# Work-ahead matmuls moved behind the attention output, exps issued behind the sines, and theta's whole turns taken off by an integer copy from ScalarE

## The chip, the cores and the metric

The kernel runs on one core of one Trainium2 chip. The metric is the device time of one execution in microseconds. The engines are TensorE (PE: matmul; PEld: its weight load), VectorE (DVE), ScalarE (ACT), GpSimd (POOL) and SyncE (SP), which issues the DMAs. Each engine works through its own instructions in the order in which they were issued, and stands still when the next one has to wait.

## The reference

Three layers, for 4 batches of 448 tokens, 12 heads of 64 and a width of 768:

```python
# attention
scores = scale * q @ k.T;  scores = where(causal mask, -1e9, scores)
attn = exp(scores - max);  attn = attn / (sum(attn) + 1e-9)
x = (attn @ v), heads side by side                    # (4, 448, 768)
# gated layer
gate_pre = causal convolution of x along the tokens, 5 taps, per channel
h = sigmoid(gate_pre) * (x @ w_val);   x = h @ w_out
# rotation layer
theta = x @ w_theta
y = w_tok_r @ (x * cos(theta)) + w_tok_i @ (x * sin(theta))   # mixes tokens
u = x + y;   out = u + max(u @ w_ch, 0)
```

## The kernel before, in words

Activations stand channels by tokens, a tile of 128x448 per sixth of the width. Each operand of a dense product is split into a high part of fewer bits and the remainder (`x_hi`, `x_lo`; `act_hi`, `act_lo`; `w_hl`), and a product is three matmuls a chunk: hi·hi, hi·lo, lo·hi. An output tile of a dense product is 36 matmuls of 448 columns (`gemm`, L535). The inputs arrive as 64-bit floats; weights are brought to 32 bits in integer arithmetic (`to_f32`, L167), split by POOL and stored for later batches.

**Attention** runs over 24 pairs of heads (`attn_iter(g)`, ten steps a pair). For pair g: `attn_T` transposes q and k, ACT copies `qt`, DVE `kt`; `attn_S` makes the scores in two groups (S0: chunks of 448, 320 and 128 columns; S1: 384, 192, 64 and 256), DVE masks them and takes the row maximum (L355), and ACT takes the exp into `prob` with the row sums (`exp_set`, L126). In the next pair's iteration `attn_PT` transposes `prob` in four parts, `attn_AV` multiplies by v, `attn_X1` scales the result into `xf`, splits it into `x_hi` (ACT, L470) and `x_lo` (POOL, L119), and `attn_X2` convolves it (for the first six pairs on POOL, L486 to L493) and takes the gate's tanh on ACT, also through `exp_set`. PSUM has two banks for dense products (`mm`) and six for all else.

**Work ahead.** Batch 0's attention (pairs 0 to 5) runs alone at the start, while the first weights are converted. There the first two output tiles of `x @ w_val` grow along, one chunk kc at a time (`gemm_ahead(kc)`, L506: 6 matmuls, L514). The loop at L732 takes one attention step for each n and issues chunk kc at n = 19, 29, ..., 69, just behind the pair's `attn_X` and so behind the first half of the next pair's program. How these matmuls are finally placed among PE's others is decided by the scheduler of the tile framework, which orders each engine's instructions by its own model of times; `tc.issue_after(ins)` forbids it to put what is under it ahead of `ins`.

**Dense work** is `dense(b)` for the batches in turn: 6 tiles of `x @ w_val` times the gate (`hf`, L573), 6 of `h @ w_out` (`x2f`), 6 of theta, then per tile the transposes of z (`ztr`, L617), the token mixing (`tok`, L638) and 6 tiles of the output. The loop at L753 interleaves the next batch's attention steps by the rates of `RATE`.

**Theta.** `theta(e)` takes theta/2π off PSUM with an ACT copy (L590), finds the whole turns by adding and taking off 12582912 on DVE (L591), takes them off (L592), and makes the absolute value on DVE in batch 0 (L594) and on ACT in the others (L598). The sine takes the signed fraction, the cosine the absolute one. After every second tile `sines(e-1)` issues four sines (two tiles; L610, L611), behind the last two exps that were issued (L606). The products with x follow on DVE (L614) and POOL or DVE (L615). ACT has the exp and the sine in different tables: between an exp or tanh and a sine there is an `ACT_TABLE_LOAD`, shown at L610 (to sines) or L127 (back to exps). The profile has 30 of them.

Of the kernel before, what the change touches and what calls it, by code (L numbers as in the profile page):

```python
# [11 lines left out]
I32 = mybir.dt.int32  # L12
U32 = mybir.dt.uint32
AF = mybir.ActivationFunctionType
ALU = mybir.AluOpType
# [3 lines left out]
MASKED = -8.0e9  # L19
INV_2PI = 1.0 / (2.0 * math.pi)  # L20
TWO_PI = 6.283185
ROUND = 12582912.0

U_DVE = (0, 1, 1, 1)
PT_DVE = (2, 4, 0, 0)
# [22 lines left out]
def kernel(  # L48
# [14 lines left out]
    nc = tc.nc  # L63
    B, H, S, D = q.shape
# [15 lines left out]
    KC = DM // P  # L80
# [22 lines left out]
    halfpi = cpool.tile([P, 1], F32, name="halfpi")  # L103
# [7 lines left out]
    def psum(tag):  # L111
        at = "mm" if tag == "mm" else "at"
        return ps.tile([P, 512], F32, tag=at, name=f"ps_{tag}", bufs=2 if tag == "mm" else 6)
# [8 lines left out]
        return nc.vector.tensor_tensor(out=dst, in0=src, in1=f32(hi), op=ALU.subtract)  # L122

    exps = []

    def exp_set(*args, **kw):  # L126
        exps.append(nc.scalar.activation(*args, **kw))  # L127

    def setup():
        make_identity(nc, ident)  # L130
# [24 lines left out]
    def setup_conv():  # L155
        t = pool.tile([P, CV, 2], I32, tag="wb", name="cv_raw", bufs=8)
        nc.sync.dma_start(
            out=t[: KW * KC, 0:P, :].rearrange("p n two -> p (n two)"),
            in_=conv_w.rearrange("k (c n) -> (k c) n", n=2 * P),
        )  # L160
        c32 = pool.tile([P, S], F32, tag="tmp", name="c32")[:, 0:P]
        to_f32(c32[: KW * KC, :], t[: KW * KC, 0:P, :])
        pt = psum("tr")
        nc.tensor.transpose(pt[:, : KW * KC], c32[: KW * KC, :], ident[: KW * KC, : KW * KC])
        nc.vector.tensor_copy(cw.rearrange("p k c -> p (k c)"), pt[:, : KW * KC])
# [118 lines left out]
    wides = {}  # L284
    ttr_ins = []
    hf_ins = []

    def load_qk(g, name):
        if g >= B * NP:
            return  # L290
        b, hp = divmod(g, NP)
        src, raw = (q, q_raw) if name == "q" else (k, k_raw)
        t = pool.tile([CP, NC, 2, D], F32, tag=f"{name}_raw", name=f"{name}_raw")
        for j in range(2):
            nc.sync.dma_start(out=t[:, :, j, :], in_=src[b, 2 * hp + j].rearrange("(c p) d -> p c d", p=CP))
        raw[g] = t
# [34 lines left out]
    def side(i, j):  # L331
        return j if 1 <= i <= 4 else 1 - j
# [50 lines left out]
    def attn_AV(g):  # L383
        if not 0 <= g < B * NP:
            return
        tv = v_raw.pop(g)
        t = pT.pop(g)
        av[g] = psum("av")
        for kc, lo, hi, n0 in SEGS:
            for j in range(2):  # L390
                o = side(lo, j) * D
                nc.tensor.matmul(  # L392
                    av[g][j * D : (j + 1) * D, lo * D : hi * D], lhsT=tv[:, j, kc, :],
                    rhs=t[:, n0 : n0 + hi - lo, o : o + D],
                    start=(kc, lo) == (0, 1), stop=kc == NC - 1, skip_group_check=True,
                )

    def attn_X(g):
        if not 0 <= g < B * NP:
            return  # L400
        attn_X1(g)
        attn_X2(g)
# [103 lines left out]
    def gemm_ahead(kc):  # L506
        xhi, xlo = x_hl[0, kc]
        g = kc // KH
        for n in range(AHEAD):
            if kc == 0:  # L510
                ahead[n] = psum("mm" if n < 2 else "tr")
            whi, wlo = splits[n, g]
            for m, (a, x) in enumerate(((whi, xhi), (whi, xlo), (wlo, xhi))):
                nc.tensor.matmul(  # L514
                    ahead[n][:, :S], lhsT=a[:, kc % KH, :], rhs=x,
                    start=kc == 0 and m == 0, stop=kc == KC - 1 and m == 2, skip_group_check=True,
                )
            if kc == KC - 1:
                splits.pop((n, 0)), splits.pop((n, 1))
# [35 lines left out]
    def dense(b):  # L555
# [8 lines left out]
        for e in range(KC):  # L564
            if b == 0 and e < AHEAD:
                pt = ahead.pop(e)
                if YLD:
                    yield
            else:
                pt = yield from gemm(xs)  # L570
# [3 lines left out]
                    out=hf, in0=gates.pop((b, e)), scalar=1.0, in1=pt[:, :S], op0=ALU.add, op1=ALU.mult  # L574
# [4 lines left out]
        for e in range(KC):  # L579
            pt = yield from gemm(h_hl)  # L580
# [5 lines left out]
        def theta(e):  # L586
            pt = yield from gemm(x2_hl)
            z = pool.tile([P, 2, S], F32, tag="z", name="z", bufs=4)
            t, kk = z[:, 1, :], z[:, 0, :]
            nc.scalar.activation(t, pt[:, :S], AF.Copy, scale=INV_2PI)  # L590
            nc.vector.tensor_scalar(out=kk, in0=t, scalar1=ROUND, scalar2=ROUND, op0=ALU.add, op1=ALU.subtract)  # L591
            nc.vector.tensor_tensor(out=t, in0=t, in1=kk, op=ALU.subtract)  # L592
            if ABS_DVE[b]:
                nc.vector.tensor_scalar(  # L594
                    out=kk.bitcast(I32), in0=t.bitcast(I32), scalar1=0x7FFFFFFF, scalar2=None, op0=ALU.bitwise_and
                )
            else:
                nc.scalar.activation(kk, t, AF.Abs)  # L598
            zri[e] = z
            if e % 2:  # L600
                sines(e - 1)
            yield

        def sines(e0):
            with ExitStack() as st:
                for ins in exps[-PIN:]:  # L606
                    st.enter_context(tc.issue_after(ins.ins))
                for e in (e0, e0 + 1):
                    t, kk = zri[e][:, 1, :], zri[e][:, 0, :]
                    nc.scalar.activation(t, t, AF.Sin, scale=TWO_PI)  # L610
                    nc.scalar.activation(kk, kk, AF.Sin, bias=halfpi, scale=-TWO_PI)  # L611
            for e in (e0, e0 + 1):
                t, kk = zri[e][:, 1, :], zri[e][:, 0, :]
                nc.vector.tensor_tensor(out=kk, in0=kk, in1=x2f[e], op=ALU.mult)  # L614
                (nc.vector if Z_DVE[b] else nc.gpsimd).tensor_tensor(out=t, in0=t, in1=x2f[e], op=ALU.mult)  # L615
# [58 lines left out]
        for e in range(KC):  # L674
            pt = yield from gemm(u_hl)
            nc.vector.scalar_tensor_tensor(
                out=x2f[e], in0=pt[:, :S], scalar=0.0, in1=x2f[e], op0=ALU.max, op1=ALU.add
# [54 lines left out]
    for n in range(5 * H + 10):  # L732
        next(at, None)
        if n == 5:
            setup_conv()
        if W_AT <= n < 5 * H:
            with tc.issue_after(ttr_ins[-1].ins):
                for at_n, (m, g) in zip(A_TILES, ((0, 0), (1, 0), (0, 1), (1, 1), (2, 0), (2, 1), (3, 0), (3, 1))):
                    if n == at_n - W_AT:
                        load_w(m, g)  # L740
                    if n == at_n:
                        stage_w(m, g)
                        if m < AHEAD + 1:
                            split_w(m, g)
        if n >= 19 and n % 10 == 9:
            gemm_ahead(n // 10 - 1)
        if n == 5 * H - 3:
            with tc.issue_after(ttr_ins[-1].ins):
                for g in range(2):
                    load_w(AHEAD + 2, g)  # L750
# [47 lines left out]
```

## Time and profile before

| | |
|---|---|
| median of three runs | 743.29 us (742.01 to 743.30) |
| the profiled execution's own time | 738.0 us |
| its span in the trace | 736.2 us |
| granted TensorE clock, mean | 0.977 |
| busy: PE, DVE, ACT, POOL | 93%, 57%, 51%, 43% of the span |

The span runs from the first to the last instruction that the profiler recorded. A granted clock of 1.0 is TensorE at 2.4 GHz, 0.5 is 1.2 GHz; a mean between is a mixture. Times in the rows are microseconds from the span's start; in square brackets stands how long the engine had been idle before the instruction, and the work that ended the wait.

### The profile page before, as it was taken

Reading aid. Unit: us, or ns where it says so; the run is one execution under the profiler, and the core shown is the slowest. Engines: PE = TensorE matmul, PEld = TensorE weight load, DVE = VectorE, ACT = ScalarE, POOL = GpSimd, SP = SyncE. Lnnn points to the kernel's source line nnn. Section 1 sums busy time; section 2 is a strip of 40 time slices with the busy share of each in tenths; the row PEclk is TensorE's granted clock in tenths of the full one; section 3 lists DMA queues with packets and bytes.
Section 4 is the critical chain, followed back from the end, with each engine's and each line's share of the span. In section 5 each row is a group of like instructions: output and inputs, shape, how many; then the busy total and the mean of one; then the engine's idle time right before and its main releaser. Section 6 shows DMA issues by size and latency. Waiting matters only on the chain.

```text
span 736.2 us, 13020 instructions
## 1 busy us (share of the span) xinstructions
PE 686.0 (93%) x4595; PEld 588.5 (80%) x4595; DVE 418.9 (57%) x1018; ACT 373.0 (51%) x853; POOL 314.4 (43%) x332
## 2 busy tenths in 40 slices
PE   5878897898899999999998999999999999999997
PEld 3655675787688888888887888888889899898996
DVE  5655689877876663644656534734578323126521
ACT  4655656775986454564864232444867212235301
POOL 1596954984757666662547200012331503102100
PEclk9897999999899999999999999999999999999999
DMA  7846346778553489888522268666431278773232
GB/s 199 193 99 187 93 134 194 246 206 302 165 157 119 124 298 307 265 286 263 158 76 62 75 200 242 185 191 201 121 88 58 64 216 233 213 209 97 86 98 63
DMA packets 133031, 124.68 MB, mean 169 GB/s; under 512 B 72905, under 2 KB 110567, under 8 KB 132967
## 3 DMA queue, kind: packets, MB, share of 16 engines
q1 hardware_dynamic: 132967, 123.86, 57.0%
q8 instruction: 36, 0.59, 0.3%
q14 instruction: 28, 0.23, 0.1%
HBM read 94.66 MB, written 29.16 MB: 168 GB/s over the span
## 4 chain that ended last, share of the span: by engine, by line
PE 62%; ACT 7%; DVE 4%; POOL 2%; DMA 1%; issue 1%; SPq 0%; DVEq 0%; ACTq 0%; POOLq 0%
PE ps_mm L535 35%; PE ps_mm L638 12%; PE ps_s L347 4%; PE ps_tr L370 3%; PE ps_av L392 3%; ACT L610 2%; PE ps_tr L624 2%; PE ps_tr L665 1%; PE ps_tr L320 1%; ACT L127 1%; ACT prob L127 1%; ACT z L610 1%; ACT z L611 1%; POOL gate L493 1%; DVE z L592 1%; DMA rb<-rows 1%
## 5 line engine op out<-in xcount | busy, mean ns | idle before, releaser
L535 PE MATMUL ps_mm<-act_hi,w_hl 128*128 128x448 f32 x864 | 268.5, 376 | 7.4 <-POOL w_hl L119 2.3
L535 PEld LDWEIGHTS ps_mm<-act_hi,w_hl 128*128 128x128 f32 x864 | 162.1, 189 | 26.1 <-POOL w_hl L119 5.7
L535 PE MATMUL ps_mm<-act_lo,w_hl 128*128 128x448 f32 x432 | 157.3, 364 | 0.0
L127 ACT ACTIVATE prob<-ps_s,negm 128x192 f32<-128x192 f32 (+6 forms) x168 | 79.3, 474 | 75.5 <-DVE negm L355 73.9
L355 DVE CUSTOM_DVE_ANT_0 ps_s<-ps_s,mask 128x192 f32<-128x192 f32 (+6 forms) x168 | 70.6, 436 | 70.1 <-PE ps_s L347 39.4
L535 PEld LDWEIGHTS ps_mm<-act_lo,w_hl 128*128 128x128 f32 x432 | 81.8, 189 | 4.5
L535 PE MATMUL ps_mm<-x_hi,w_hl 128*128 128x448 f32 x264 | 82.6, 379 | 0.6 <-DVE hf L573 0.4
L119 POOL TENSOR_TENSOR act_lo<-x2f,act_hi 128x448 fp32r<-128x448 f32 x36 | 41.8, 1161 | 75.8 <-ACT act_hi L549 26.3
L119 POOL TENSOR_TENSOR w_hl<-cv_raw,w_hl 128x384 fp32r<-128x384 f32 x62 | 65.3, 1054 | 18.7 <-ACT w_hl L248 17.1
L119 POOL TENSOR_TENSOR x_lo<-xf,x_hi 128x448 fp32r<-128x448 f32 x23 | 29.5, 1283 | 97.5 <-ACT x_hi L470 97.5
L638 PE MATMUL ps_mm<-wtok_h,zt_h 128*128 128x448 f32 x168 | 64.7, 385 | 2.0 <-ACT zt_h L629 1.9
L638 PE MATMUL ps_mm<-wtok_h,zt_l 128*128 128x448 f32 x168 | 63.3, 379 | 2.4 <-DVE zt_l L122 2.4
L638 PE MATMUL ps_mm<-wtok_l,zt_h 128*128 128x448 f32 x168 | 62.4, 372 | 0.0
L347 PE MATMUL ps_s<-kt,qt 64*64 64x256 f32 (+6 forms) x672 | 57.3, 416 | 4.9 <-ACT x_hi L470 1.3
L493 POOL TENSOR_TENSOR gate<-gate,tp 128x448 f32<-128x448 f32 x48 | 58.4, 1217 | 2.3
L615 POOL TENSOR_TENSOR z<-z,x2f 128x448 f32<-128x448 f32 x18 | 21.9, 1219 | 85.4 <-ACT z L610 85.4
L370 PE MATMUL ps_tr<-ident,prob 128*128 128x128 f32 x384 | 56.2, 285 | 1.4 <-ACT prob L127 1.4
L347 PEld LDWEIGHTS ps_s<-kt,qt 64*64 64x64 f32 x672 | 30.6, 140 | 32.3 <-issue 18.9
L535 PEld LDWEIGHTS ps_mm<-x_hi,w_hl 128*128 128x128 f32 x264 | 50.4, 192 | 6.3 <-DVE hf L573 0.9
L370 PEld LDWEIGHTS ps_tr<-ident,prob 128*128 128x128 f32 x384 | 47.2, 146 | 7.0 <-ACT prob L127 1.8
L392 PEld LDWEIGHTS ps_av<-pt,v 128*64 128x64 f32 x768 | 41.0, 140 | 12.9 <-DVE cv_raw L177 3.0
L392 PE MATMUL ps_av<-pt,v 128*64 128x64 f32 (+3 forms) x768 | 48.8, 281 | 2.6 <-DVE cv_raw L177 2.6
(106 smaller groups left out, 1185.8 us busy)
## 6 DMA issues: line engine op xcount, KB each, us to landing
w_hl<-scratch SPq DMA_DIRECT2D x120, 384.0 KB
scratch<-w_hl SPq DMA_DIRECT2D x48, 384.0 KB
q_raw<-in_q_dram SPq DMA_DIRECT2D x48, 112.0 KB
k_raw<-in_k_dram SPq DMA_DIRECT2D x48, 112.0 KB
out_dram<-o SPq DMA_DIRECT2D x24, 224.0 KB
v<-in_v_dram SPq DMA_DIRECT2D x48, 96.0 KB
cv_raw<-in_moe_w_val_dram SPq DMA_DIRECT2D x12, 384.0 KB
plain<-cv_raw SPq DMA_DIRECT2D x24, 192.0 KB
```

What stands on the lines that cost most here:

```text
L119: nc.gpsimd.tensor_tensor(out=dst, in0=src, in1=f32(hi), op=ALU.subtract)
L127: exps.append(nc.scalar.activation(*args, **kw))
L347: nc.tensor.matmul(bank[o : o + D, off : off + n], lhsT=qt[j * D : (j + 1) * D, i * D : (i + 1) * D], rhs=kt[j * D : (j + 1) * D, :n], sta ...
L355: ttr = nc.vector.tensor_tensor_reduce(out=pt, in0=pt, in1=mask[:, S - n : S], scale=-1.0 / math.sqrt(D), scalar=3.0e38, op0=ALU.add, op1= ...
L370: nc.tensor.transpose(pt[:, n * P : (n + 1) * P], probs[i][:, kc * P : (kc + 1) * P], ident)
L392: nc.tensor.matmul(av[g][j * D : (j + 1) * D, lo * D : hi * D], lhsT=tv[:, j, kc, :], rhs=t[:, n0 : n0 + hi - lo, o : o + D], start=(kc, l ...
L493: nc.gpsimd.tensor_tensor(out=gt, in0=gt, in1=tp, op=ALU.add)
L535: nc.tensor.matmul(pt[:, :S], lhsT=a[:, kc % KH, :], rhs=x, start=kc == 0 and m == 0, stop=kc == KC - 1 and m == 2,)
L610: nc.scalar.activation(t, t, AF.Sin, scale=TWO_PI)
L615: (nc.vector if Z_DVE[b] else nc.gpsimd).tensor_tensor(out=t, in0=t, in1=x2f[e], op=ALU.mult)
L624: nc.tensor.transpose(pt[:, (m - m0) * P : (m - m0 + 1) * P], z.rearrange("p a s -> p (a s)")[:, m * P : (m + 1) * P], ident,)
L638: nc.tensor.matmul(pt[:, :S], lhsT=a[:, m, :], rhs=w[:, m, :], start=m == 0 and n == 0, stop=m == NZ - 1 and n == 2,)
```

## The change

Three parts.

1. **Work ahead.** Chunks 0 to 4 are issued at n = 24, 34, 44, 54, 64 and no longer at 19, 29, ..., 59, and not ahead of the last matmul of the attention output (`attn_AV`) that stands in the program at that point. Chunk 5 stays at n = 69.
2. **Exps behind sines.** Every exp and tanh that goes through `exp_set` once a sine has been issued may not be put ahead of the latest cosine.
3. **Theta.** The ACT copy off PSUM writes theta/2π as int32, so that the conversion rounds to whole turns. One DVE instruction then computes theta/2π from PSUM once more and takes the integer off. The add-and-subtract of 12582912 (L591) is gone, 24 instructions in all.

On PE, part 1 shows at every pair of the first stage. Before, around pair 1, the chunk stands between the transposes of `prob` and the next scores:

```order
L370 MATMUL ps_tr<-ident,prob_77 128x128 x4
L370 MATMUL ps_tr<-ident,prob_72 128x128
L370 MATMUL ps_tr<-ident,prob_75 128x128 x3
L514 MATMUL ps_mm<-x_hi,w_ahead 128x448 x2
L347 MATMUL ps_s<-kt,qt 64x448 x2
L347 MATMUL ps_s<-kt,qt 64x320 x2
```

Now the whole chunk stands behind the attention output, ahead of the transposes of the next q and k:

```order
L396 MATMUL ps_av<-pt,v_79 64x128 x2
L396 MATMUL ps_av<-pt,v_79 64x64 x2
L396 MATMUL ps_av<-pt,v_79 64x128 x2
L396 MATMUL ps_av<-pt,v_79 64x64 x2
L519 MATMUL ps_mm<-x_hi,w_ahead 128x448
L519 MATMUL ps_mm<-x_lo,w_ahead 128x448
L519 MATMUL ps_mm<-x_hi,w_ahead 128x448 x2
L519 MATMUL ps_mm<-x_lo,w_ahead 128x448
L519 MATMUL ps_mm<-x_hi,w_ahead 128x448
L324 MATMUL ps_tr<-ident,q_raw 128x112 x4
L324 MATMUL ps_tr<-ident,k_raw 128x112 x4
```

The six matmuls of a chunk are one block now; before, two of them stood here and four behind the next part of `prob`.

On ACT, part 2 shows at the first sines of each of the batches 0, 1 and 2. In batch 0, before (L610 and L611 are sine and cosine, L127 the exps of S1):

```order
L176 ACTIVATE cv_raw<-cv_raw 128x384
L610 ACT_TABLE_LOAD
L610 ACTIVATE z<-z 128x448
L611 ACTIVATE z<-z,halfpi 128x448
L127 ACT_TABLE_LOAD
L127 ACTIVATE prob_73,sums<-ps_s,negm 128x192
L127 ACTIVATE prob_71,sums<-ps_s,negm 128x64
L610 ACT_TABLE_LOAD
L610 ACTIVATE z<-z 128x448
L611 ACTIVATE z<-z,halfpi 128x448
L127 ACT_TABLE_LOAD
L127 ACTIVATE prob_74,sums<-ps_s,negm 128x256
```

Now (L616 and L617 are sine and cosine, L130 the exps, L595 the copy of theta):

```order
L595 ACTIVATE z<-ps_mm 128x448
L616 ACT_TABLE_LOAD
L616 ACTIVATE z<-z 128x448
L617 ACTIVATE z<-z,halfpi 128x448
L179 ACTIVATE cv_raw<-cv_raw 128x384
L616 ACTIVATE z<-z 128x448
L617 ACTIVATE z<-z,halfpi 128x448
L130 ACT_TABLE_LOAD
L130 ACTIVATE prob_76,sums<-ps_s,negm 128x384
L130 ACTIVATE prob_73,sums<-ps_s,negm 128x192
L130 ACTIVATE prob_71,sums<-ps_s,negm 128x64
L130 ACTIVATE prob_74,sums<-ps_s,negm 128x256
```

Four table loads became two, and all four exps of S1 stand behind all four sines. ACT's order as a whole has 20 table loads and no longer 30: 4 fewer in batch 0, 2 in batch 1, 4 in batch 2. In the batches 0 and 2 a gate's tanh between later sines has moved behind them in the same way.

The diff:

```diff
--- before.py
+++ after.py
@@ -19,7 +19,6 @@
 MASKED = -8.0e9
 INV_2PI = 1.0 / (2.0 * math.pi)
 TWO_PI = 6.283185
-ROUND = 12582912.0
 
 U_DVE = (0, 1, 1, 1)
 PT_DVE = (2, 4, 0, 0)
@@ -122,9 +121,13 @@
         return nc.vector.tensor_tensor(out=dst, in0=src, in1=f32(hi), op=ALU.subtract)
 
     exps = []
+    sins = []
 
     def exp_set(*args, **kw):
-        exps.append(nc.scalar.activation(*args, **kw))
+        with ExitStack() as st:
+            if sins:
+                st.enter_context(tc.issue_after(sins[-1].ins))
+            exps.append(nc.scalar.activation(*args, **kw))
 
     def setup():
         make_identity(nc, ident)
@@ -284,6 +287,7 @@
     wides = {}
     ttr_ins = []
     hf_ins = []
+    av_ins = []
 
     def load_qk(g, name):
         if g >= B * NP:
@@ -389,11 +393,12 @@
         for kc, lo, hi, n0 in SEGS:
             for j in range(2):
                 o = side(lo, j) * D
-                nc.tensor.matmul(
+                mm = nc.tensor.matmul(
                     av[g][j * D : (j + 1) * D, lo * D : hi * D], lhsT=tv[:, j, kc, :],
                     rhs=t[:, n0 : n0 + hi - lo, o : o + D],
                     start=(kc, lo) == (0, 1), stop=kc == NC - 1, skip_group_check=True,
                 )
+        av_ins.append(mm)
 
     def attn_X(g):
         if not 0 <= g < B * NP:
@@ -587,9 +592,10 @@
             pt = yield from gemm(x2_hl)
             z = pool.tile([P, 2, S], F32, tag="z", name="z", bufs=4)
             t, kk = z[:, 1, :], z[:, 0, :]
-            nc.scalar.activation(t, pt[:, :S], AF.Copy, scale=INV_2PI)
-            nc.vector.tensor_scalar(out=kk, in0=t, scalar1=ROUND, scalar2=ROUND, op0=ALU.add, op1=ALU.subtract)
-            nc.vector.tensor_tensor(out=t, in0=t, in1=kk, op=ALU.subtract)
+            nc.scalar.activation(kk.bitcast(I32), pt[:, :S], AF.Copy, scale=INV_2PI)
+            nc.vector.scalar_tensor_tensor(
+                out=t, in0=pt[:, :S], scalar=INV_2PI, in1=kk.bitcast(I32), op0=ALU.mult, op1=ALU.subtract
+            )
             if ABS_DVE[b]:
                 nc.vector.tensor_scalar(
                     out=kk.bitcast(I32), in0=t.bitcast(I32), scalar1=0x7FFFFFFF, scalar2=None, op0=ALU.bitwise_and
@@ -608,7 +614,7 @@
                 for e in (e0, e0 + 1):
                     t, kk = zri[e][:, 1, :], zri[e][:, 0, :]
                     nc.scalar.activation(t, t, AF.Sin, scale=TWO_PI)
-                    nc.scalar.activation(kk, kk, AF.Sin, bias=halfpi, scale=-TWO_PI)
+                    sins.append(nc.scalar.activation(kk, kk, AF.Sin, bias=halfpi, scale=-TWO_PI))
             for e in (e0, e0 + 1):
                 t, kk = zri[e][:, 1, :], zri[e][:, 0, :]
                 nc.vector.tensor_tensor(out=kk, in0=kk, in1=x2f[e], op=ALU.mult)
@@ -742,8 +748,11 @@
                         stage_w(m, g)
                         if m < AHEAD + 1:
                             split_w(m, g)
-        if n >= 19 and n % 10 == 9:
-            gemm_ahead(n // 10 - 1)
+        if n >= 24 and n % 10 == 4:
+            with tc.issue_after(av_ins[-1].ins):
+                gemm_ahead(n // 10 - 2)
+        if n == 5 * H + 9:
+            gemm_ahead(KC - 1)
         if n == 5 * H - 3:
             with tc.issue_after(ttr_ins[-1].ins):
                 for g in range(2):
```

## Rows read from the trace of the kernel before

**Rows 1.** the page, part 1: engine, busy us, share of the span, instructions

```profile
PE 686.0 (93%) x4595; PEld 588.5 (80%) x4595; DVE 418.9 (57%) x1018; ACT 373.0 (51%) x853; POOL 314.4 (43%) x332
```

**Rows 2.** PE's waits: line <- releaser: us in total, times, longest

```profile
PE ps_mm L514 <- ACT x_hi L470: 6.3, 5, 2.3
...
PE ps_mm L514 <- POOL x_lo L119: 5.0, 2, 3.0
...
PE ps_mm L638 <- DVE zt_l L122: 2.4, 4, 0.8
...
PE ps_tr L624 <- DVE z L614: 1.6, 1, 1.6
```

**Rows 3.** windows: PE, PEld, DVE, ACT, POOL busy us, PE clock, DMA share, GB/s

```profile
28.00:62.00 34.00, 29.20 (x242) 21.32 (x243) 20.44 (x61) 18.96 (x55) 32.74 (x39) 0.85 0.42 111
...
68.00:94.00 26.00, 20.58 (x191) 15.65 (x191) 15.82 (x49) 15.70 (x45) 24.33 (x29) 0.93 0.44 108
...
192.00:196.00 4.00, 3.15 (x11) 2.21 (x12) 4.00 (x10) 3.98 (x9) 3.85 (x5) 0.67 0.86 260
...
196.00:200.00 4.00, 4.00 (x21) 3.62 (x21) 3.23 (x8) 3.99 (x8) 3.33 (x4) 0.90 0.25 98
```

**Rows 4.** POOL in time: start us, us, instruction [idle before <-releaser]

```profile
61.07 1.13 POOL L493 TENSOR_TENSOR gate<-gate,tp 128x448 f32<-128x448 f32 x1
...
68.61 0.64 POOL L486 TENSOR_SCALAR gate<-xf,cw 128x448 f32<-128x448 f32 x1 [6.40 <-DMA q_raw<-in_q_dram]
...
91.42 1.13 POOL L119 TENSOR_TENSOR x_lo<-xf,x_hi 128x448 fp32r<-128x448 f32 x1
```

**Rows 5.** ACT in time, attention of pair 4

```profile
62.23 0.58 ACT L127 ACTIVATE gate<-gate 128x448 f32<-128x448 f32 x1 [0.70 <-POOL gate L493]
```

**Rows 6.** ACT in time, first sines of batch 0

```profile
181.14 1.28 ACT L610 ACT_TABLE_LOAD   x1
...
185.30 0.31 ACT L127 ACTIVATE prob<-ps_s,negm 128x64 f32<-128x64 f32 x1
...
188.16 1.28 ACT L127 ACT_TABLE_LOAD   x1
...
189.46 0.47 ACT L127 ACTIVATE prob<-ps_s,negm 128x256 f32<-128x256 f32 x1
```

**Rows 7.** PE in time, at the same place

```profile
185.75 1.06 PE L624 MATMUL ps_tr<-ident,z 128*128 128x128 f32 x7 [2.08 <-ACT prob L127]
...
192.34 0.27 PE L419 MATMUL ps_tr<-ident,rec 128*7 128x128 f32 x1 [1.40 <-DVE rec L409]
...
193.07 0.88 PE L624 MATMUL ps_tr<-ident,z 128*128 128x128 f32 x4 [0.47 <-ACT qt L325]
...
194.00 0.74 PE L638 MATMUL ps_mm<-wtok_h,zt_h 128*128 128x448 f32 x1
```

**Rows 8.** DVE groups: xcount | busy us, mean ns | idle before

```profile
L591 DVE TENSOR_SCALAR z<-z 128x448 f32<-128x448 f32 x24 | 10.7, 447 | 12.2 <-ACT z L590 12.0
...
L592 DVE TENSOR_TENSOR z<-z 128x448 f32<-128x448 f32 x24 | 17.4, 725 | 0.3
...
L573 DVE SCALAR_TENSOR_TENSOR hf<-gate,ps_mm 128x448 f32<-128x448 f32 x24 | 14.8, 615 | 31.8 <-PE ps_mm L535 27.3 <-PE ps_mm L514 3.0 <-POOL w_hl L119 1.2
...
L614 DVE TENSOR_TENSOR z<-z,x2f 128x448 f32<-128x448 f32 x24 | 23.0, 959 | 24.2 <-ACT z L611 24.2
```

**Rows 9.** ACT groups, the copy that scales theta and another cast

```profile
L590 ACT ACTIVATE z<-ps_mm 128x448 f32<-128x448 f32 x24 | 12.9, 536 | 11.4 <-PE ps_mm L535 11.3
...
L470 ACT CAST x_hi<-xf 128x448 fp32r<-128x448 f32 x24 | 13.7, 570 | 27.6 <-DVE xf L465 27.5
```

**Rows 10.** ACT in time, first sines of batch 1

```profile
349.97 0.53 ACT L590 ACTIVATE z<-ps_mm 128x448 f32<-128x448 f32 x1
...
353.53 0.31 ACT L127 ACTIVATE prob<-ps_s,negm 128x64 f32<-128x64 f32 x1
```

**Rows 11.** PE in time, batch 1, transposes of z

```profile
356.21 0.93 PE L624 MATMUL ps_tr<-ident,z 128*128 128x128 f32 x7
```

## The prediction

> **What bounds the kernel now.** I read the busy shares first: PE is busy for 686.0 of 736.2 us [rows 1], so PE's idle time, 50 us, is all that a better order can give back, and nothing in the change takes a matmul away. The list of PE's waits says where that idle time is [rows 2]: 11.3 us of it at L514, the work-ahead chunks, which wait for the pair's x_hi (6.3) and x_lo (5.0); 2.4 us at L638, token mixing, which waits for the low half of z's transposes; 1.6 us at L624 behind the products with x. Each of the three parts of the change aims at one of these. Then I read which engine is last behind PE in those places, by stage [rows 3] and in order of time [rows 4 to 7, 10, 11].
>
> In the attention stage it is POOL: busy 32.74 of the 34 us from 28 to 62, and 24.33 of the 26 from 68 to 94, while PE is busy 29.20 and 20.58 [rows 3]. At the first sines of batch 0 it is ACT: 3.98 of 4 us from 192 to 196. Those two places are the whole case; from about 200 us on PE has nearly no gaps but the few small ones below.
>
> **Part 1, the work ahead.** It removes nothing: six matmuls a chunk stay, five chunks of them go behind the attention output. The 11.3 us of waits at L514 would go, since a pair's x_hi and x_lo are ready long before the next pair's attention output is done. But a wait that goes is paid only if what comes next is not late as well. Next is the scores' exps, and ACT is held, in order, by the gate's tanh, which waits for POOL's convolution: for one pair it ended at 62.20 (61.07 + 1.13) [rows 4] and ACT started the tanh at 62.23 after 0.70 us of waiting for it [rows 5]. POOL does the same work in the same order as before, and it has no gap over 0.5 us but one, the 6.40 us ahead of 68.61 [rows 4]. That gap is the chain from the tanh over the next exps, their transposes, the attention output and xf: it starts when POOL is done, and no chunk of the work ahead stands in its way that was not ready. The stage ends for the dense work with x_lo of the last pair, at 91.42 + 1.13 on POOL [rows 4]; chunk 5, which is not moved, waits for just that. So I take **0** for this part. Below: if POOL's one gap shrank by the two longest waits, 2.3 and 3.0 us [rows 2], 5.3 us. Above: the block of six now stands ahead of q's and k's transposes; at 201 ns a matmul (the distance of two at full clock; L638 starts at 194.00 [rows 7] in the same shape) it delays them by 1.2 us, by 2.2 at half clock, and if nothing covers that at five pairs it is 6 us. What covers it is that qt and kt are wanted only after DVE has made xf, which waits for ACT and POOL.
>
> **Part 2, exps behind sines.** Ten table loads go, 1.28 us each [rows 6], 12.8 us of ACT. ACT is busy for 373.0 us of the span [rows 1], so only what lies in the places where ACT is last counts.
>
> Batch 0. Before, ACT goes to the sine table at 181.14, back for the exps of 192 and 64 columns, to the sines, and back again at 188.16, so that the last exp (256 columns) starts at 189.46 [rows 6]. PE meets this in four places [rows 7]: 2.08 us ahead of the transposes of z at 185.75, which wait for the exp of 64 columns; 1.40 at 192.34 for the reciprocal of the row sums, which need the last exp; 0.47 at 193.07 for qt, which stands behind them on ACT. The granted clock from 192 to 196 is 0.67 and then 0.90 [rows 3].
> - In the new order that exp of 64 comes behind all four sines but saves one load; earlier by 1.28 (a load) and by some 1.3 (the DVE work of part 3, which the sines wait for), later by two sines (about 1.1) and the exps of 384 and 192 columns (about 0.9). It is about level: 0.3 us gained.
> - The last exp is earlier by two loads and the DVE work, 2.57 + 1.3 = 3.9 us. That covers 1.40 + 0.47: **1.87 us** gained.
> - The clock: a mean of 0.67 over 4 us is 2.64 us at the half level, 0.90 is 0.8 us. PE is busy 3.15 of 4 and 4.00 of 4 there, so 2.08 + 0.8 us of work at half speed would take half as long at full: **1.44 us**. Taken whole, because PE stood still twice just ahead of it; nothing is its lower bound.
>
> The Trainium skill (ScalarE: Activation LUTs, What ACT_TABLE_LOAD costs) prices a switch of tables at 1283 ns and a drain of 1380 ns on top, 2.66 us in all. By it the ten loads would be 26.6 us of ACT and batch 0's last exp would come 2.8 us earlier still, with the same 1.87 us for PE. The trace shows the 1.28 and no drain: the exp of 256 starts at 189.46, 0.02 us after the load from 188.16 has ended.
>
> Batches 1 to 3. The waits of L638 for zt_l, four in number, 2.4 us [rows 2], lie behind the first pairs of sines in batch 1 and batch 2, where ACT loses two and four loads ahead of the copies that zt_l is made from: **2.4 us**, all of it, since each wait is under one load. L624's 1.6 us for z in batch 3 has no exps beside it; the DVE instruction that goes gives 0.4 of it.
>
> **Part 3, theta.** Removed: 24 DVE instructions of 447 ns, 10.7 us. Of two, L591 and L592 (725 ns), one is left, which reads PSUM and an integer [rows 8]. Its price is not in the trace; the nearest row is L573, the same form off PSUM, 615 ns; the ends are 447 (L591) and 959 (L614), and I take 615. For the ACT copy that writes integers the nearest are L590 itself, 536, and L470, 570, a copy that changes the type [rows 9]; I take 536. DVE is busy 57% of the span [rows 1], so all of this is hidden but where the sines wait for it, and there it is counted above. PSUM's bank is held by about 0.6 us longer, until the DVE instruction has read it; with two banks and a gemm of 36 x 0.2 = 7.2 us between, that is covered. Four places on the path times 0.34 (959 − 615) makes 1.4 us of doubt each way.
>
> **Sum.** 0 + 0.3 + 1.87 + 1.44 + 2.4 + 0.4 = 6.4 us. The profiled execution took 738.0, so it would take 731.6; the three runs shown have a median of 743.29, 5.3 us (0.7%) above it. I forecast for the runs: 743.3 − 6.4 = **736.9 us**, −0.9%. A measurement of this kernel tells about 0.2%, 1.5 us, from no change. With nothing for the clock and 1.4 for theta it is 3.6 us (739.7), with theta's 1.4 the other way and half of part 1's lower bound 10.5 (732.8).
>
> **Rivals.**
> - *Attention pays too.* POOL's gap of 6.40 us [rows 4] speaks for it: POOL is not the limit there. If the two longest waits at L514 bring the next xf earlier, 5.3 us come on top: about 731.5. Against it: the tanh that ACT waits for at 62.23 [rows 5] is POOL's, and not moved. 0.14.
> - *Nothing arrives.* ACT's freed time is behind DVE, which converts weights in the same stretch (batch 0), or POOL is last with its products with x (3.85 of 4 us from 192 to 196 [rows 3]); and the small waits come back one instruction on. Then −1 to +1 us: about 743. 0.13.
> - *The exps come too late.* This is the other sign, and one mechanism: S1's exps stand behind four sines, so its scores hold their PSUM banks and PE, in order, stops at the transposes of z, which take the next bank. In batch 1 PE starts them at 356.21 without a wait [rows 11]; the exp of 64 columns was done at 353.84 [rows 10]. In the new order the second tile's copy ends at 350.50 [rows 10]; with L614's product ahead on DVE (until 351.2), the new DVE instruction, the absolute value, two sines, a load and the exps of 384, 192 and 64 columns (0.62 + 0.56 + 0.58 + 0.65 + 1.28 + 0.5 + 0.4 + 0.3) the exp ends at about 356.1. That is the point it decides from: every us of later sines is a us of PE, in each of three batches, and a product on DVE beside POOL's, or a bank held by theta, is worth one to two. With 2.5 us a batch it is 7.5, less 4 us of the gains that stay: about 747. 0.15.
> - That the change doesn't do what it says (the copy to integers leaves theta with another rounding) costs or gives no time.
>
> **How the numbers follow.** The forecast, a gain of 3 to 9 us, has 0.58; the four add to 1. Low end: the first rival's 731.5; high end: no change, 743.5, which leaves out the slower rival and little else. Faster by over 0.2% is forecast plus first rival, 0.72; within 0.2% 0.13; slower 0.15. The forecast's own range is 734 to 740.
>
> **What would show it.** Table loads 20. L591's group gone and the new one near 615 ns. PE's waits: no L514 behind x_hi and x_lo but the last chunk's, the attention stage still ending near 93 us; the wait at the reciprocal in batch 0 gone, the granted clock from 190 to 200 near 1; no wait of L638 for zt_l. It is wrong if the stage up to 94 us is shorter by over 2 us (first rival), if new waits of L624 for prob show in batches 1 and 2 (third), or if PE's idle time is still near 50 us (second).

## The result and the profile after

The changed kernel takes **730.25 us** (median of four runs, 729.67 to 731.59) against 743.29 us (742.01 to 744.59): a ratio of 0.9827, 95% interval 0.9805 to 0.9849, or 13.0 us less. Timed once more, beside other runs of before, it had 0.9838 (0.9811 to 0.9864). The forecast was 736.9, its low end 731.5. The direction was right; the gain was twice the forecast, and the time lies 1.25 us under the range.

The first trace of before came from an execution of 738.0 us, 5 us shorter than its runs, so the two traces differ by 7.5 us only. A second trace of before (span 741.6, first experiment) stands beside it in the table below. Its columns are distances between starts of instructions on DVE and ACT: the first `hf` of batch 0 (end of the attention stage), its last `x2f` copy, the first output instruction of each batch (L676 before), and the last one.

| us | to first hf | to last x2f | to first output | batch 1 | batch 2 | rest |
|---|---|---|---|---|---|---|
| before, first trace | 93.4 | 69.0 | 89.0 | 169.5 | 164.0 | 145.2 |
| before, second trace | 97.4 | 69.6 | 89.8 | 169.6 | 163.9 | 145.2 |
| the change | 96.5 | 70.9 | 84.0 | 165.3 | 161.5 | 144.7 |
| the change, second trace | 96.2 | 72.5 | 84.8 | 165.3 | 161.4 | 144.6 |
| part 1 | 96.0 | 70.7 | 90.3 | 170.0 | 163.0 | 145.2 |
| part 2 | 96.4 | 69.0 | 89.9 | 168.5 | 162.0 | 145.2 |
| part 3 | 95.5 | 69.8 | 88.6 | 167.3 | 163.3 | 144.7 |
| parts 1 and 2 | 95.9 | 71.4 | 89.2 | 167.1 | 161.6 | 145.2 |
| parts 1 and 3 | 94.6 | 71.6 | 89.8 | 167.3 | 163.3 | 144.6 |
| parts 2 and 3 | 94.8 | 71.2 | 84.5 | 165.4 | 161.4 | 144.6 |
| PSUM operand only | 99.3 | 70.9 | 88.4 | 168.4 | 162.9 | 144.8 |
| one DVE instruction less only | 98.3 | 70.9 | 87.5 | 169.5 | 162.9 | 145.2 |
| part 2, PSUM operand only | 94.8 | 71.1 | 87.1 | 167.2 | 161.6 | 144.6 |
| part 2, one DVE instruction less only | 96.3 | 71.7 | 84.5 | 168.1 | 161.5 | 145.0 |
| the change, loads back in batch 0 | 94.1 | 70.4 | 86.8 | 165.3 | 161.7 | 144.6 |
| the change, loads back in batches 1, 2 | 94.3 | 70.6 | 86.2 | 166.8 | 163.7 | 144.6 |

The first two columns scatter from one execution to the next: by 4.0 us in the first between the two traces of before, by 1.6 in the second between the two of the change. The other four carry the result: 5.0 us at batch 0's theta and mixing, 4.3 in batch 1, 2.5 in batch 2, 0.6 behind it, means of two traces each. That is 12.3 before rounding, about what the runs show.

The page of the change, engines, answers to [rows 1]:

```profile
PE 684.8 (94%) x4595; PEld 588.4 (81%) x4595; DVE 409.1 (56%) x994; ACT 360.5 (49%) x843; POOL 310.6 (43%) x332
```

ACT lost 12.5 us, DVE 9.8 and POOL, whose work nobody touched, 3.8. The waits of PE that answer to [rows 2], and the two longest that are new (all of the change; us in total, times, longest):

```profile
PE ps_s L351 <- DVE cv_raw L180: 5.2, 1, 5.2
PE ps_s L351 <- ACT qt L329: 5.0, 2, 2.8
...
PE ps_mm L644 <- ACT zt_h L635: 1.6, 2, 0.8
PE ps_mm L519 <- POOL x_lo L118: 1.2, 1, 1.2
...
PE ps_tr L630 <- DVE z L620: 0.8, 1, 0.8
```

L514's 11.3 us became 1.5 at L519, and the attention stage is no shorter: PE now stops at the next scores (L351), for qt and, once, behind an instruction of DVE's weight conversion. Token mixing (L644) has no wait for zt_l any more.

The prices of the new instructions, groups of the change on DVE and ACT, answering to [rows 8, 9]:

```profile
L596 DVE SCALAR_TENSOR_TENSOR z<-ps_mm,z 128x448 f32<-128x448 f32 x24 | 14.7, 614 | 13.3 <-ACT z L595 13.3
```

```profile
L595 ACT ACTIVATE z<-ps_mm 128x448 int32<-128x448 f32 x24 | 12.9, 539 | 16.8 <-PE ps_mm L540 16.8
```

At the first sines of batch 0, windows of before's second trace and then of the change (length, busy us of PE, PEld, DVE, ACT, POOL, granted clock, DMA share, GB/s):

```profile
190.00:195.00 5.00, 3.86 (x16) 3.52 (x17) 2.68 (x6) 4.93 (x10) 1.95 (x2) 0.70 0.88 213
195.00:200.00 5.00, 3.00 (x13) 1.94 (x12) 4.56 (x11) 5.00 (x12) 4.61 (x5) 0.84 0.69 198
200.00:205.00 5.00, 5.00 (x24) 4.32 (x23) 4.22 (x11) 4.97 (x10) 4.24 (x6) 0.78 0.38 140
...
405.00:410.00 5.00, 3.09 (x8) 2.56 (x9) 3.11 (x8) 3.02 (x7) 1.87 (x2) 0.70 0.01 2
410.00:415.00 5.00, 5.00 (x29) 4.58 (x29) 2.09 (x7) 1.67 (x6) 0.72 (x1) 0.95 0.02 3
```

```profile
190.00:195.00 5.00, 4.04 (x22) 2.96 (x20) 4.81 (x11) 4.98 (x12) 3.83 (x4) 1.00 1.10 275
195.00:200.00 5.00, 4.54 (x24) 3.98 (x25) 4.91 (x11) 4.92 (x9) 3.76 (x4) 1.00 0.66 236
200.00:205.00 5.00, 5.00 (x27) 3.16 (x26) 4.82 (x9) 4.62 (x8) 3.88 (x5) 1.00 0.44 132
...
400.00:405.00 5.00, 5.00 (x30) 4.66 (x29) 3.59 (x11) 2.39 (x7) 0.41 (x1) 1.00 0.02 3
```

The clock, 0.70 to 0.84 before, is whole in both traces of the change. The last two rows of before are the end of batch 1, where it also falls, behind a wait that the forecast passed over; the change has 1.00 there (its last row).

### The profile page after: what moved, and what is told of

Same layout as the page of the kernel before. It is cut to its first block, busy times and chain, and to the rows that moved or that the text cites. A ratio compares the mean times of both kernels' runs of the same rounds, so it can differ in the third digit from the quotient of the medians.

```text
span 728.7 us, 13007 instructions
## 1 busy us (share of the span) xinstructions
PE 684.8 (94%) x4595; PEld 588.4 (81%) x4595; DVE 409.1 (56%) x994; ACT 360.5 (49%) x843; POOL 310.6 (43%) x332
## 4 chain that ended last, share of the span: by engine, by line
PE 79%; DVE 9%; ACT 4%; POOL 2%; issue 2%; DMA 2%; SPq 2%; DVEq 0%; ACTq 0%; POOLq 0%
PE ps_mm L540 43%; PE ps_mm L644 14%; PE ps_s L351 6%; PE ps_tr L374 5%; PE ps_av L396 4%; PE ps_tr L630 2%; DVE ps_cv L173 2%; PE ps_tr L324 1%; PE ps_tr L671 1%; DVE ps_cv L176 1%; ACT prob L130 1%; SPq L299 1%; DVE ps_s L359 1%; DVE cv_raw L180 1%; DMA cv_raw<-in_moe_w_val_dram 1%
## 5 line engine op out<-in xcount | busy, mean ns | idle before, releaser
L130 ACT ACTIVATE prob<-ps_s,negm 128x192 f32<-128x192 f32 (+6 forms) x168 | 79.4, 474 | 74.3 <-DVE negm L359 73.3
L359 DVE CUSTOM_DVE_ANT_0 ps_s<-ps_s,mask 128x192 f32<-128x192 f32 (+6 forms) x168 | 70.6, 435 | 74.2 <-PE ps_s L351 42.1
L351 PE MATMUL ps_s<-kt,qt 64*64 64x256 f32 (+6 forms) x672 | 60.5, 430 | 16.7 <-DVE cv_raw L180 5.2
L351 PEld LDWEIGHTS ps_s<-kt,qt 64*64 64x64 f32 x672 | 31.9, 144 | 44.3 <-issue 17.4
L644 PE MATMUL ps_mm<-wtok_h,zt_h 128*128 128x448 f32 x168 | 64.0, 381 | 1.6 <-ACT zt_h L635 1.6
L644 PE MATMUL ps_mm<-wtok_h,zt_l 128*128 128x448 f32 x168 | 62.3, 372 | 0.1
L644 PE MATMUL ps_mm<-wtok_l,zt_h 128*128 128x448 f32 x168 | 61.3, 365 | 0.0
L498 POOL TENSOR_TENSOR gate<-gate,tp 128x448 f32<-128x448 f32 x48 | 55.9, 1165 | 2.3
```

The source lines that it names most:

```text
L351: nc.tensor.matmul(bank[o : o + D, off : off + n], lhsT=qt[j * D : (j + 1) * D, i * D : (i + 1) * D], rhs=kt[j * D : (j + 1) * D, :n], sta ...
L359: ttr = nc.vector.tensor_tensor_reduce(out=pt, in0=pt, in1=mask[:, S - n : S], scale=-1.0 / math.sqrt(D), scalar=3.0e38, op0=ALU.add, op1= ...
L498: nc.gpsimd.tensor_tensor(out=gt, in0=gt, in1=tp, op=ALU.add)
L644: nc.tensor.matmul(pt[:, :S], lhsT=a[:, m, :], rhs=w[:, m, :], start=m == 0 and n == 0, stop=m == NZ - 1 and n == 2,)
```

## The experiments

Theory S, after the first comparison: the sines carry the gain, and the work ahead nothing. Theory A: the work ahead carries what the forecast missed.

**Before once more.**

> The kernel before once more, unchanged. Theory S (the sines carry the gain, and the profiled execution of before, 738.0 us, was 5 us short in the attention stage by chance): this run takes 742 to 745 us and its trace reaches the first hf of batch 0 some 3 to 5 us later than the 93.4 us of the first trace, everything behind being alike. Theory A (the work ahead carries the rest): the attention stage is again near 93 us, and the 5 us between the profiled execution and the median lie elsewhere, at a lower granted clock.

742.30 us, ratio 1.0009 (0.9982 to 1.0036). The first hf came at 97.4 us and no longer at 93.4; of the 5.3 us between the two traces of before, 4.0 lie there. As theory S had it.

**Part 1 alone** (the diff's `av_ins` and `gemm_ahead` lines).

> Part 1 alone, the work ahead behind the attention output; exps and theta as before. Theory S: no gain, between -1 and +3 us (the first hf of batch 0 at 93 to 97 us), because POOL and then x_lo of the last pair set the end of the stage. Theory A: -5 us or more.

742.06 us, ratio 0.9996 (0.9977 to 1.0015). No gain. Theory A falls. Part 1's trace shows what came in place of a wait at L514, PE in time: the next scores wait for qt, a thing that PE did not reach so early before:

```profile
40.33 1.34 PE L348 MATMUL ps_s<-kt,qt 64*64 64x448 f32 x6 [3.00 <-ACT qt L326]
```

**Part 2 alone** (`sins`, `exp_set`).

> Part 2 alone, exps and tanh behind the sines, 20 table loads for 30. Theory S: -7 to -11 us, spread as -4 at the sines of batch 0, -4 to -5 in batch 1, -2 in batch 2. Theory A: -4 us or less, about what the sum on record gave it (5.7).

736.48 us, ratio 0.9919 (0.9888 to 0.9951), −6.0 us. Batch 1 gained 1.0 and batch 2 1.9, but batch 0's sines nothing: ACT, rid of two loads, stood 3.28 us for DVE ahead of them, and PE then 2.81 for the reciprocal (ACT in time, then PE):

```profile
184.32 0.58 ACT L180 ACTIVATE cv_raw<-cv_raw 128x384 f32<-128x384 f32 x1 [3.28 <-DVE ps_cv L174]
184.93 1.28 ACT L614 ACT_TABLE_LOAD   x1
```

```profile
195.33 0.27 PE L423 MATMUL ps_tr<-ident,rec 128*7 128x128 f32 x1 [2.81 <-DVE rec L413]
```

**Part 3 alone** (theta's copy and subtraction).

> Part 3 alone, the integer copy; 28 table loads by the order of ACT. Theory S and theory A: -1 to -2 us, since DVE is last only in front of the sines of batch 0 and of batch 3. The new instruction on DVE takes 0.6 us (0.45 to 0.96), ACT's copy 0.54.

737.50 us, ratio 0.9937 (0.9917 to 0.9957), −4.7 us: over twice what both theories gave it. In batch 0 the exps among the sines now came late and PE stopped 3.36 us for `prob`, and 1.74 and 1.26 us in batches 1 and 2, where before had no such stop; the gain was in batch 1 all the same, 2.3 us. So a second question: what joins the two parts in batch 0, and what does part 3 do in batch 1. Theory C: together they take the clock's fall away, which either alone leaves. Theory D: each gives its own.

**Parts 2 and 3.**

> Parts 2 and 3 together, the work ahead as before. Part 2 alone measured -5.4 us and part 3 alone -4.4 (medians), part 1 alone 0. Theory C (the two together take the clock's fall at batch 0's first sines away, which either alone leaves: windows of 0.50 to 0.70 there): -12 to -13 us, all of the change; granted clock 1.00 from 185 to 205, and -4 to -6 us between the last x2f and the last out of batch 0. Theory D (each part gives its own and nothing together): -10 us or less, a clock below 0.9 somewhere in that stretch.

729.73 us, ratio 0.9825 (0.979 to 0.9859): the whole change, without part 1. Batch 0's sines gain 4.9 us where each part alone gave 1 or less, and the clock there is 1.00 from 180 to 210. That is theory C, though a trace further down shows the fall once more in the order of the change. Parts 1 with 3, and 1 with 2, complete the pairs:

> Parts 1 and 3, exps as before. Theory C and theory D: -4 to -5 us, as part 3 alone. If the work ahead is what makes the rest, more than -7.

737.05 us, ratio 0.9913 (0.9877 to 0.995), as part 3 alone.

> Parts 1 and 2, theta as before. Theory C and theory D: -5 to -6 us, as part 2 alone; the wait of token mixing for zt_h at the end of batch 1 (1.9 us) stays and the clock falls behind it, as in part 2 alone.

738.09 us, ratio 0.9929 (0.9902 to 0.9956), as part 2 alone. Part 1 gives nothing in any company. One point of the expectation was missed: the wait for zt_h at the end of batch 1 stays, 1.94 us as in part 2 alone, but the clock behind it does not fall (PE in part 2 alone, then in parts 1 and 2):

```profile
404.19 0.47 PE L642 MATMUL ps_mm<-wtok_h,zt_h 128*128 128x448 f32 x1 [1.94 <-ACT zt_h L633]
```

```profile
405.42 0.47 PE L644 MATMUL ps_mm<-wtok_h,zt_h 128*128 128x448 f32 x1 [1.94 <-ACT zt_h L635]
```

Windows of the same two traces: behind the wait, and all of batch 1 (columns as in [rows 3], with the length in front).

```profile
405.00:410.00 5.00, 5.00 (x17) 4.52 (x18) 2.76 (x9) 2.20 (x8) 0.00 (x0) 0.67 0.00 0
...
255.33:423.86 168.53, 166.24 (x1136) 143.05 (x1135) 94.83 (x225) 89.16 (x210) 95.75 (x92) 0.99 0.65 202
```

```profile
405.00:410.00 5.00, 4.52 (x21) 3.89 (x22) 3.58 (x10) 3.26 (x10) 0.37 (x1) 1.00 0.00 0
...
256.53:423.60 167.07, 164.77 (x1136) 141.77 (x1135) 93.97 (x224) 89.15 (x210) 95.64 (x92) 1.00 0.66 204
```

PE stands idle for 2.3 us of batch 1 in both (length less busy time). The 1.5 us between them are what the fallen clock costs.

**The table loads by themselves.** The order of the change is kept on every engine; only this is added, in batch 0 or in batches 1 and 2:

```diff
+                    if b == 0 and e == 1:
+                        st.enter_context(tc.issue_after(sins[-1].ins))
+                        one = pool.tile([P, 1], F32, tag="one", name="one", bufs=1)
+                        d = nc.scalar.activation(one, halfpi, AF.Exp)
+                        st.enter_context(tc.issue_after(d.ins))
                     nc.scalar.activation(t, t, AF.Sin, scale=TWO_PI)
```

> All three parts, and two of the table loads put back in batch 0: a one-column exp stands between the two pairs of the first sines, and every other instruction of every engine is in the order of the change. ACT's work there is 2.6 us longer plus 0.3 us for the exp (left in, it feeds nothing). Theory L (the loads are on the path there, and a stop of PE of some 3 us costs as much again by the clock): batch 0's -5 us falls to between 0 and -2, the granted clock from 190 to 205 falls below 0.9, total -8 to -10 us against before. Theory M (the order of the exps makes the gain, DVE is last there and covers the loads): unchanged, -12 to -13 us.

732.03 us, ratio 0.9866 (0.9831 to 0.99), −10.0 us: some 2 us of the gain go, at the edge of what theory L gave; the interval overlaps that of the change. The wait of the forecast's third rival appears, and the clock from 190 to 195 is 0.71. PE in time:

```profile
186.50 0.60 PE L635 MATMUL ps_tr<-ident,z 128*128 128x128 f32 x4
189.56 0.90 PE L635 MATMUL ps_tr<-ident,z 128*128 128x128 f32 x3 [2.06 <-ACT prob L130]
```

> All three parts, and two table loads put back in batch 1 and two in batch 2 in the same way, between the pairs of the first sines; nothing else moves. Theory L: PE's waits return (for the exps of 64 columns ahead of z's transposes, or of token mixing for zt_l), 1 to 2.5 us in each of the two batches: -8 to -11 us in total against before. Theory M: unchanged, -12 to -13 us.

733.83 us, ratio 0.9884 (0.9851 to 0.9917): 3 to 4 us go, as theory L had it. Batch 1 is 1.5 us longer and batch 2 2.3, each with a new wait for the exp of 64 columns, 1.30 and 1.31 us. Ahead of batch 1 this kernel is the change itself, with the same order on every engine and the same two small waits of PE at the first sines (0.82 and 0.41 us). Yet its clock falls there, and its first output comes after 86.2 us, not 84.0 or 84.8 (a window of this trace):

```profile
195.00:200.00 5.00, 5.00 (x20) 4.36 (x19) 4.76 (x10) 4.58 (x10) 4.85 (x5) 0.67 0.24 90
```

So that column scatters by 1 to 2 us, and the order of the change does not keep the clock whole each time. Batch 0's price of the loads is shown as a wait of 2.06 us; its size in the total is not clear of the noise.

**What part 3 is made of.** It takes a DVE instruction away, and it lets the other read one operand from PSUM. Theory E: the second matters, because DVE instructions with two SBUF inputs slow POOL's convolution. Theory F: the first. Two kernels have one each. The PSUM operand alone:

```diff
-            nc.vector.tensor_tensor(out=t, in0=t, in1=kk, op=ALU.subtract)
+            nc.vector.scalar_tensor_tensor(
+                out=t, in0=pt[:, :S], scalar=INV_2PI, in1=kk, op0=ALU.mult, op1=ALU.subtract
+            )
```

> Of part 3 only that the subtraction reads theta from PSUM; the add-and-subtract of 12582912 stays, so DVE has as many instructions as before. Theory E (shared access: DVE instructions with two SBUF inputs slow POOL's beside them; before, POOL's additions of the convolution took 1.53 and 1.62 us beside L592 and L614, 1.15 alone): the wait for zt_h at the end of batch 1 shrinks from 1.94 to about 1.3 us or less, POOL's L493 mean from 1217 to some 1170 ns, total -2 to -3 us. Theory F (one DVE instruction fewer ahead of ACT and POOL is what counts): no gain, -1 to +1 us, the wait at 1.9.

739.83 us, ratio 0.9969 (0.9947 to 0.9991), −2.3 us, as theory E had it. The wait for zt_h shrank from 1.9 to 1.3 (PE's waits in before's second trace, then in this kernel):

```profile
PE ps_mm L638 <- ACT zt_h L629: 1.9, 1, 1.9
```

```profile
PE ps_mm L640 <- ACT zt_h L631: 1.3, 1, 1.3
```

POOL's additions went from 1216 to 1161 ns (groups of POOL, the same two traces):

```profile
L493 POOL TENSOR_TENSOR gate<-gate,tp 128x448 f32<-128x448 f32 x48 | 58.4, 1216 | 2.3
```

```profile
L493 POOL TENSOR_TENSOR gate<-gate,tp 128x448 f32<-128x448 f32 x48 | 55.7, 1161 | 2.3
```

One DVE instruction fewer alone, its time put on ACT:

```diff
-            nc.vector.tensor_scalar(out=kk, in0=t, scalar1=ROUND, scalar2=ROUND, op0=ALU.add, op1=ALU.subtract)
-            nc.vector.tensor_tensor(out=t, in0=t, in1=kk, op=ALU.subtract)
+            nc.scalar.activation(kk.bitcast(I32), pt[:, :S], AF.Copy, scale=INV_2PI)
+            nc.vector.tensor_tensor(out=t, in0=t, in1=kk.bitcast(I32), op=ALU.subtract)
```

> Of part 3 only that DVE has one instruction fewer: ACT writes theta/2pi in float and, in a second copy, as an integer; DVE subtracts the one from the other, both from SBUF (24 more ACT copies of 0.54 us). Theory E (sharing with POOL matters beside the instruction count): the gain of part 3 (-4.4) shrinks to -2 or less, the convolution's additions on POOL stay at 1.2 us, and the wait for zt_h at the end of batch 1 is near 1.3 to 1.9 us. Theory F (one DVE instruction fewer is the gain): -3 to -4.5 us, the wait at 0.8.

739.65 us, ratio 0.9959 (0.9927 to 0.9991), −3.0 us, which is theory F's time, with the wait for zt_h still at 1.7, which is theory E's. The same two edits beside part 2:

> Part 2, and of part 3 only that the subtraction reads PSUM (as many DVE instructions as before). Parts 2 and 3 together gave -12.7 us, part 2 alone -6.0. Theory E (most of part 3 is that POOL's convolution beside it is no longer slowed): -9 to -11 us; the convolution's additions on POOL at 1165 ns, the wait for zt_h at the end of batch 1 at 1.3 or less. Theory F (most of part 3 is the instruction that goes): -6 to -8 us, and a wait of over 2 us at batch 0's first sines.

734.34 us, ratio 0.9894 (0.9875 to 0.9914).

> Part 2, and of part 3 only that DVE has one instruction fewer, with both operands of the other in SBUF (ACT makes a second copy). Theory E: -6 to -8 us, the additions on POOL at 1200 ns or more, the wait for zt_h at 1.7 to 1.9. Theory F: -9 to -12 us.

734.37 us, ratio 0.9891 (0.9871 to 0.9911).

> The change once more, for a second trace on the chip of these two. Both theories: -12 to -13.5 us; the first hf of batch 0 anywhere between 93.4 and 99.3 us, the scatter of the eleven traces so far, since part 1 does not set it.

730.94 us, ratio 0.9838 (0.9811 to 0.9864). Part 2 alone was −6.0; each half of part 3 adds 2, both together 6 to 7. Neither theory holds for the whole: both halves count. Where each counts rests on single traces. At batch 0's sines it is 84.5 us with one DVE instruction less, as in the whole change, and 87.1 with the PSUM operand only; that column scatters by 1 to 2 us. In batch 1 the lengths (168.1 and 167.2) do not rank the halves, because the clock fell in the first trace and not in the second. PE's idle time there does better: 2.3 us with part 2, 1.8 with the DVE instruction less, 1.6 with the PSUM operand, 0.8 with both. The scheduler places some other instructions anew in each of these four kernels, so their sizes are less sure than those of the two with the loads put back.

## Why the prediction was wrong

**Part 1, 0 forecast: right.** The waits at L514 went and other waits of PE came; the end of the stage is set elsewhere. The first rival named the time nearest to the measured one (731.5 us) by chance, with the wrong mechanism: attention did not pay.

**The prices: right.** 614 ns measured for the new DVE instruction, 615 taken; 539 for the copy, 536 taken; 1.28 us a load. Loads are 20. The drain that the Trainium skill adds to a load (ScalarE: Activation LUTs, What ACT_TABLE_LOAD costs) does not show here either. With loads put back, the one-column exp starts 0.01 us after the load has ended, ACT in time:

```profile
182.37 1.28 ACT L619 ACT_TABLE_LOAD   x1
183.66 0.20 ACT L619 ACTIVATE one<-halfpi 128x1 f32<-128x1 f32 x1
```

**Batch 0, 3.6 us forecast, 5.0 measured.** The step "It is about level: 0.3 us gained" failed. PE's wait for the exp of 64 columns (2.30 us in before's second trace) went altogether, for two reasons.

The exp comes 1.1 us earlier, not 0.3: from the end of theta's second copy to its start it is 8.0 us in both traces of before and 6.9 in both of the change. The step's terms were wrong. No load is saved ahead of this exp, for two stand ahead of it in either order; the exp of 192 columns stood ahead of it before as well; and the exp of 384, put on ACT's bill in full, costs little, since ACT stood idle for DVE just ahead of it before and spends this time on sines now. ACT of before's second trace, then of the change:

```profile
182.13 0.54 ACT L590 ACTIVATE z<-ps_mm 128x448 f32<-128x448 f32 x1
185.07 0.58 ACT L127 ACTIVATE prob<-ps_s,negm 128x384 f32<-128x384 f32 x1 [2.40 <-DVE negm L355]
...
190.69 0.31 ACT L127 ACTIVATE prob<-ps_s,negm 128x64 f32<-128x64 f32 x1
```

```profile
181.76 0.54 ACT L595 ACTIVATE z<-ps_mm 128x448 int32<-128x448 f32 x1
182.31 1.28 ACT L616 ACT_TABLE_LOAD   x1
...
188.15 0.58 ACT L130 ACTIVATE prob<-ps_s,negm 128x384 f32<-128x384 f32 x1
...
189.18 0.31 ACT L130 ACTIVATE prob<-ps_s,negm 128x64 f32<-128x64 f32 x1
```

And PE needs it later. Before, all seven transposes of z's first tile stand behind this exp; in the change four start ahead of it, at 188.91, and only the last three stand behind it. It is so in every trace with part 2 and in none without: the first four wait for DVE with it, for ACT without it. The forecast held the order of PE for given. PE of before's second trace, then of the change:

```profile
191.14 0.98 PE L624 MATMUL ps_tr<-ident,z 128*128 128x128 f32 x7 [2.30 <-ACT prob L127]
...
197.72 0.27 PE L419 MATMUL ps_tr<-ident,rec 128*7 128x128 f32 x1 [1.39 <-DVE rec L409]
198.46 0.80 PE L624 MATMUL ps_tr<-ident,z 128*128 128x128 f32 x4 [0.47 <-ACT qt L325]
```

```profile
188.91 0.60 PE L630 MATMUL ps_tr<-ident,z 128*128 128x128 f32 x4
...
189.76 0.49 PE L630 MATMUL ps_tr<-ident,z 128*128 128x128 f32 x3
...
194.31 0.47 PE L644 MATMUL ps_mm<-wtok_h,zt_h 128*128 128x448 f32 x1 [0.82 <-ACT zt_h L635]
...
195.40 0.55 PE L630 MATMUL ps_tr<-ident,z 128*128 128x128 f32 x3 [0.42 <-DVE cv_raw L180]
```

The three waits there, 4.2 us in before's second trace (2.30, 1.39, 0.47), are now 0.82 and 0.42: 2.9 us. The 2.1 that remain are left to the clock, a remainder and not a measurement: windows of 0.70, 0.84 and 0.78 are 6.8 us at the half level, and 4.2 us of work in them would give 2.1. The forecast had 1.4 for it. That the parts need each other here is what it missed most: ACT is last only once DVE is not, so part 2 alone and part 3 alone leave PE standing some 3 us (2.81 and 3.36), and the clock falls behind that.

**Batches 1 to 3, 2.8 us forecast, 7.3 measured.** The sentence that failed is "from about 200 us on PE has nearly no gaps but the few small ones". It passed over the wait at the end of batch 1, in before's second trace 1.94 us of token mixing for zt_h, and the clock behind it (0.70 in the window from 405). The 2.4 us for zt_l came as forecast: all four waits went. The chain of the wait for zt_h: ACT's copies to zt_h stand behind a gate's tanh, the tanh behind POOL's convolution, and that had instructions of 1.53 and 1.62 us among others of 1.14. ACT of before's second trace, then of the change:

```profile
405.81 0.58 ACT L127 ACTIVATE gate<-gate 128x448 f32<-128x448 f32 x1 [1.79 <-POOL gate L493]
```

```profile
397.42 0.58 ACT L130 ACTIVATE gate<-gate 128x448 f32<-128x448 f32 x1 [0.61 <-POOL gate L498]
```

POOL of the same two traces:

```profile
395.63 1.53 POOL L493 TENSOR_TENSOR gate<-gate,tp 128x448 f32<-128x448 f32 x1
...
397.99 1.62 POOL L493 TENSOR_TENSOR gate<-gate,tp 128x448 f32<-128x448 f32 x1
```

```profile
387.81 1.16 POOL L498 TENSOR_TENSOR gate<-gate,tp 128x448 f32<-128x448 f32 x1
...
390.17 1.15 POOL L498 TENSOR_TENSOR gate<-gate,tp 128x448 f32<-128x448 f32 x1
```

The slow ones lie, by their times, beside the subtraction of theta (L592) and the product with x (L614), both with two SBUF inputs (DVE of before's second trace):

```profile
395.22 0.93 DVE L592 TENSOR_TENSOR z<-z 128x448 f32<-128x448 f32 x1
...
397.97 0.62 DVE L614 TENSOR_TENSOR z<-z,x2f 128x448 f32<-128x448 f32 x1 [1.35 <-ACT z L611]
```

The wait fell to 0.76 us, worth 1.2, and the clock stayed whole: 3.5 us at the half level before (windows of 0.70 and 0.95), up to 1.75; the two kernels above with equal idle time put it at 1.5. With the two waits for zt_l, 1.2, that makes 3.9 to 4.1 of batch 1's 4.3. Batch 2 gave 2.5, of which waits that went (0.71, 0.39, 0.48) make 1.6, all of PE's idle time there; the other 0.9 is no idle time, the granted clock is 1.00 on both sides, and it stays unexplained. Batch 3 gave 0.6, forecast 0.4.

**The rivals.** "Nothing arrives" fell. "The exps come too late" fell, but it was near: in batch 1 of the change the exp of 64 columns ends at 355.88, where 356.1 was worked out. With two loads put back, which is 2.6 us of later sines, PE stands 1.3 us at that place in batches 1 and 2 and 2.1 in batch 0; with part 3 alone it stands there too.

Open: why the first transposes of z no longer wait for the exp once part 2 is in; why the clock falls behind one stop and not behind an equal one; and what sets the scatter of the first 165 us, in which no part shows a gain.

## What to carry to other kernels

Price an edit at every place where it occurs, and list PE's waits by every releaser before calling a stretch free of gaps: the one wait of 1.9 us that was left out held over a quarter of batch 1's gain and the clock behind it a third or more. Where two engines take turns at being last, as at batch 0's sines, an edit on either alone shows little there; try them together before dropping one. An edit to one engine's order can change what another engine waits for; compare the waits of all of them before working out a gain. A wait that goes is a gain only if the next releaser is early: 11.3 us of waits went at the work ahead for nothing.

## What the runs showed of the hardware

An engine that the change does not touch became faster: POOL's convolution additions went from 1216 to 1161 ns in the mean when one DVE instruction in 24 places read PSUM in place of SBUF (no other edit, though the scheduler placed some instructions anew); they took 1200 ns where it kept both inputs in SBUF and DVE had one instruction fewer. The Trainium skill (SBUF — State Buffer, Who interferes with whom) says that a DVE instruction with two SBUF inputs contends with a GpSimd instruction that reads SBUF, and one with at most one, outside DVE's two-port modes, does not; these runs agree. In the two meetings with the product with x at the end of batch 1 the later one pays: before, the product with x started 0.02 us ahead of POOL's addition and took 0.62 us, the addition 1.62; with the PSUM operand alone the addition started 0.05 us ahead (399.39 against 399.44) and took 1.15, the product 1.58.

The length of a stop of PE does not settle alone what the clock does behind it. At the end of batch 1, six of the seven traces that stop there for 1.72 to 1.94 us for zt_h show the half level behind it (0.70 in before's second trace, 0.67 with part 2 alone), and parts 1 and 2 show 1.00 behind 1.94 us. None of the nine that stop for 0.75 to 1.33 us shows a fall. With the stop the same, the fall cost 1.5 us of 168.5.
